# Attention with routed experts on one core: the packed chunks' splits on ScalarE and VectorE, and the value products put off by one unit

## The chip, the cores and the metric

The kernel runs on one core of a Trainium2 chip. The metric is device microseconds of one execution, the median of several runs; smaller is better. Beside the runs there is one profiled execution, whose trace gives every row shown below. Engines are TensorE (PE in the rows), VectorE (DVE), ScalarE (ACT), GpSimd (POOL) and SyncE (SP).

## What is computed

Attention over 4 batches, 8 heads, 576 positions of 64 numbers, mixed with a read of a memory matrix, and a mixture of experts over its 2304 output rows: 8 experts, of which each row takes two.

```python
scores = np.where(causal, -1e9, scale * q @ k.T);  a = softmax(scores);  local = a @ v
q_p = np.where(q > 0, q, np.exp(q) - 1.0) + 1.0
mem_out = (q_p @ M_prev) / ((q_p * z_prev).sum(-1) + 1e-06)
x = g * mem_out + (1 - g) * local                  # g = sigmoid(beta), rows of 512
logits = x @ w_gate + log1p(exp(x @ w_noise)) * noise
for each row: its two best experts e, softmax of the two logits as weights
out[row] += weight * (max(x[row] @ w1[e], 0) @ w2[e])
```

Products are made in pieces: a number is split into a rounded part ("hi") and what is left ("lo"), and hi·hi, lo·hi and hi·lo are added up.

## The kernel before

**Chunks and units.** The 576 positions of a batch are five chunks: i = 0 to 3 hold 128 rows of all 8 heads; i = 4 holds the last 64 rows and is *packed*: two heads share the 128 partitions. A chunk is worked off in units: two of four heads for i < 2, else four of two heads; 64 units in all. For a packed chunk the query parts are `q4h` and `q4l`; the key parts are the last 64 columns of `kT`, of which all the batch's later units read as well.

**One unit.** `score` multiplies queries and keys on TensorE (line 528, or 519 for a packed chunk), adds the mask, and takes the row maximum on VectorE (L538). `expo` takes the exponential on ScalarE (L559). `trans` turns the result `a` over on TensorE into a PSUM tile `tpa` (L577), up to four blocks to a tile, and ScalarE copies it to `aT` (L578). `av` multiplies `aT` with the values on TensorE (L599, `avT`, which uses half of the array's columns). After a chunk's last unit `out_copy` (L608, ScalarE) brings `avT` to `xo`, and `out_turn` turns it over (L635, `tpo`), scales it (L637) and adds the memory's part `xm` (L639) on VectorE.

**The loop over units.** Iteration u issues `expo(u+1)` and then mixes two lists. `ys` has the products and masks of `score(u+2)`, an `out_turn` that was put off, `av(u-1)` and perhaps an `out_copy`. `xs` has the preparation of later chunks, the routing of the finished ones and `trans(u)`. So each engine has one fixed order, on which it works in turn; an instruction that waits holds everything behind it on its engine.

**Preparation of a chunk.** `k_turn` and `q_turn` turn keys and queries over on TensorE (L409); ScalarE copies them to `kf` (L416) and `qf` (L441). For all but the first chunks GpSimd then makes the parts: the hi casts (L421 for `kT`, L452 for `qh` and `q4h`) and the lo subtractions (L422, L454). `mem` ends with the multiplication that gives `xm`, on GpSimd (L476).

**Routing.** When all of a batch's rows are known, `routing` finds each row's places in the experts' tables and puts ten indirect scatters of 16-byte rows on GpSimd's queue (L282, in a list `puts`). They are issued while the next batch is worked on, and on GpSimd's queue they stand directly ahead of the key parts of that batch's packed chunk. Batches 1, 2 and 3 have such scatters in front of their packed chunk; batch 0 has none.

**Experts.** From about 304 us on the experts' products (L906, L919) run on TensorE.

Of the kernel before, what the change touches and what calls it, by code (L numbers as in the profile page):

```python
# [9 lines left out]
F32 = mybir.dt.float32  # L10
# [5 lines left out]
ALU = mybir.AluOpType  # L16
# [3 lines left out]
P = 128  # L20
# [26 lines left out]
def tile_attention_moe(ctx: ExitStack, tc: tile.TileContext, q, k, v, M_prev, z_prev, beta,  # L47
                       w_gate, w_noise, noise, w1, w2, out):
    nc = tc.nc
# [269 lines left out]
    def attention():  # L319
        with ExitStack() as c2:  # L320
            ap_ = c2.enter_context(tc.tile_pool(name="ap", bufs=2))
# [70 lines left out]
            def prep(c):  # L392

                b, i = chunks[c]
                n = rows_of(i)
                d = CH.setdefault(c, {"b": b, "i": i, "n": n})
# [21 lines left out]

                def k_split():
                    hi, lo = keys()  # L420
                    (nc.gpsimd.tensor_copy if c > 1 else nc.scalar.copy)(hi, d["kf"])  # L421
                    nc.gpsimd.tensor_tensor(out=lo, in0=d["kf"], in1=hi.bitcast(F32), op=ALU.subtract)  # L422

                def turn_first(nm, g0):

# [21 lines left out]
                def q_split(part):  # L447
                    for j in ([0, 1] if i == 4 else [None]):
                        a = slice(0, P) if j is None else slice(j * 64, j * 64 + 64)
                        hi, lo = [d[nm][a, :, a] for nm in ("qh", "ql")]  # L450
                        if part == 0:
                            (nc.gpsimd.tensor_copy if c > 1 else nc.scalar.copy)(hi, d["qf"][a])  # L452
                        else:
                            nc.gpsimd.tensor_tensor(out=lo, in0=d["qf"][a], in1=hi.bitcast(F32), op=ALU.subtract)  # L454

                def q_min():
                    d["qpT"] = ap_.tile([P, 4, P], F32, tag="qpT", name="qpT", bufs=2)
# [2 lines left out]
                def mem(g0):  # L460
                    if g0 == 0:
                        d["xm"] = ap_.tile([P, H, D], F32, tag="xm", name="xm", bufs=4)
                    tp = ps_tp.tile([P, 512], F32, tag="tp", name="tpm")
                    v_ = tp[0:n, 0:4 * 65].rearrange("p (h e) -> p h e", e=65)
                    for g in range(2):
                        nc.tensor.matmul(tp[0:n, g * 130:(g + 1) * 130], d["qpT"][:, g0 + g, 0:n],
                                         mz[:, b, g0 + g].rearrange("p a e -> p (a e)"), start=True, stop=True)
                    m_ = ap_.tile([P, 4 * 65], F32, tag="mm", name="mm", bufs=3)
                    nc.scalar.copy(m_[0:n], tp[0:n, 0:4 * 65])
                    v_ = m_[0:n].rearrange("p (h e) -> p h e", e=65)  # L470
                    r = ap_.tile([P, 4, 1], F32, tag="mr", name="mr", bufs=4)
                    hs = slice(2 * g0, 2 * g0 + 4)
                    nc.vector.scalar_tensor_tensor(out=r[0:n], in0=v_[:, :, 64:65], scalar=1e-6, in1=ig[0:n, hs].unsqueeze(2),
                                                   op0=ALU.add, op1=ALU.mult)
                    nc.vector.reciprocal(r[0:n], r[0:n])
                    nc.gpsimd.tensor_tensor(out=d["xm"][0:n, hs, :], in0=v_[:, :, 0:64],  # L476
                                            in1=r[0:n].to_broadcast([n, 4, 64]), op=ALU.mult)

                mm = [lambda: mem(0), lambda: mem(2)]
# [11 lines left out]
            units = [(c, hs) for c in range(len(chunks)) for hs in units_of(chunks[c][1])]  # L491
# [72 lines left out]
            def trans(u):  # L564
                c, hs = units[u]
                i = CH[c]["i"]
                st = U[u]
                a = st["a"]
                aT = ap_.tile([P, 8, P], F32, tag="aT", name="aT", bufs=3)
                st["aT"] = aT  # L570
                nblk = len(hs) * (i + 1) if i < 4 else 5

                def bank(g):
                    w = min(4, nblk - g)
                    tp = ps_tp.tile([P, 512], F32, tag="tp", name="tpa")
                    for x_ in range(w):
                        nc.tensor.transpose(tp[:, x_ * P:(x_ + 1) * P], a[:, (g + x_) * P:(g + x_ + 1) * P], ident)  # L577
                    nc.scalar.copy(aT[:, g:g + w, :].rearrange("p b t -> p (b t)"), tp[:, 0:w * P])  # L578

                return [lambda g=g: bank(g) for g in range(0, nblk, 4)]  # L580

            def av(u):

                c, hs = units[u]
                d = CH[c]
                i, n = d["i"], d["n"]
                aT = U[u]["aT"]
                c0 = c - i

                def pairs():  # L590
                    if hs[0] == 0:
                        d["av"] = ps_av.tile([P, 512], F32, tag="avT", name="avT", bufs=1)
                    o_ = d["av"].rearrange("p (g t) -> p g t", g=4)
                    for h0 in sorted(h for h in hs if h % 2 == 0):
                        for j in range(i + 1):
                            for k_ in range(2):
                                x_ = hs.index(h0 + k_)
                                r_ = aT[:, j, x_ * 64:(x_ + 1) * 64] if i == 4 else aT[:, x_ * (i + 1) + j, :]
                                nc.tensor.matmul(o_[k_ * 64:(k_ + 1) * 64, h0 // 2, 0:n], CH[c0 + j]["v"][:, h0 + k_, :], r_,  # L599
                                                 start=(j == 0), stop=(j == i))  # L600
                return [pairs]
# [57 lines left out]
            NU = len(units)  # L659
# [63 lines left out]
                if c == 3:  # L723
                    late_consts()

            late = deque()
            for u in range(NU + 1):
                if u + 1 < NU:
                    expo(u + 1)
                ys = score(u + 2) if u + 2 < NU else []  # L730
                if u >= 1:
                    if late:
                        ys.append(late.popleft())
                    ys += av(u - 1)
                    cl = units[u - 1][0]
                    if u == NU or units[u][0] != cl:
                        ys.append(lambda cl=cl: out_copy(cl))
                        late.append(lambda cl=cl: out_turn(cl))
                xs = []
                if u < NU:  # L740
                    c, hs = units[u]
                    if u == first[c]:
                        on_chunk(c)
                    if chunks[c] == (B - 1, 4) and u == first[c]:
                        for f in range(2):
                            W0.append(load_w(None, 0, f, None, None, [
                                ap_.tile([P, H, D], F32, tag=nm + "n", name="w0" + nm, bufs=4) for nm in "kq"]))
                    if chunks[c] == (B - 1, 4) and u == first[c] + 1:
                        W0[:] = [split_w(ep, W0[0], "a", 1), split_w(ep, W0[1], "b", 1)]
                    if chunks[c][1] == 4 and (u + 1 == NU or units[u + 1][0] != c):  # L750
                        xs.append(lambda c=c: sums(c))
                    la = 4 if u < 3 else 7
                    nxt = units[u + la][0] if u + la < NU else -1
                    while any(f[0] <= nxt for f in fills):
                        xs.append(fills.popleft()[1])
                    while ev and ev[0][0] < TU[u + 1]:
                        xs.append(ev.popleft()[2])
                    for _ in range(1 if c < len(chunks) - 1 else 2):
                        if xq:
                            xs.append(xq.popleft())  # L760
                    if len(xq) > 2:
                        xs.append(xq.popleft())
                    if puts:
                        xs.append(lambda: puts and puts.popleft()())
                    xs += trans(u)
                    if puts:
                        xs.append(lambda: puts and puts.popleft()())
                nx, ny = len(xs), len(ys)
                done = 0
                for y, f in enumerate(ys):  # L770
                    f()
                    if small:
                        small.popleft()()
                    while done * ny < (y + 1) * nx:
                        xs[done]()
                        done += 1
                        if small:
                            small.popleft()()
                for f in xs[done:]:
                    f()  # L780
            d = CH[len(chunks) - 1]
            while late or xq:
                (late or xq).popleft()()
            return (list(small)
                    + xt_logits(d["b"], d["i"], d["x"].rearrange("p h d -> p (h d)")) + routing(B - 1, 3, 5))

# [408 lines left out]
```

## Time and profile before

| | |
|---|---|
| median of 3 runs | 773.23 us (770.99 to 773.27) |
| the profiled execution, its own time | 774.38 us |
| its span in the trace | 772.7 us |
| mean granted TensorE clock | 0.962 |
| busy in the span | PE 715.3 us (93%), DVE 418.0, ACT 371.3, POOL 366.2 |

The trace's span leaves out 1.7 us of the profiled execution's own time. That time is 1.15 us above the median. A granted clock of 1.00 is the higher of TensorE's two levels (2.4 GHz), 0.50 the lower (1.2 GHz); a value between them is a mean over a stretch.

### The profile page before, as it was taken

How to read it: one execution, taken by the hardware profiler on the slowest of the kernel's cores; microseconds unless marked ns; L12 is line 12 of the kernel's file. 1: busy time of each engine (PE TensorE's matmuls, PEld its weight loads, DVE VectorE, ACT ScalarE, POOL GpSimd, SP SyncE). 2: the span in 40 equal slices, each digit the busy share in tenths (PEclk: the TensorE clock that was granted, in tenths of full speed). 3: DMA queues.
4: the chain of work that ended last, by engine and by line, in shares of the span. 5: the costliest groups of instructions: out<-in, count | busy, mean ns of one | idle time of the engine just before them, and what ended most of it. 6: DMA issues, size and time to landing. Idle time of an engine off the chain costs nothing. (4 is left out here: it accounts for less than half of the span.)

```text
span 772.7 us, 14495 instructions
## 1 busy us (share of the span) xinstructions
PE 715.3 (93%) x5166; PEld 612.0 (79%) x5166; DVE 418.0 (54%) x1053; ACT 371.3 (48%) x951; POOL 366.2 (47%) x400
## 2 busy tenths in 40 slices
PE   6999996999699968878999999999999999999993
PEld 4678774877587757767888888988889988889882
DVE  3557583669377736826446454454554555455212
ACT  5588874787478744215415335234244244253210
POOL 6334527543664451555353572662752753724502
PEclk8799997999899989998999999999999999999998
DMA  9664421251120014659557465584683693864301
GB/s 166 89 131 98 106 73 37 63 103 55 36 78 21 16 57 130 152 93 241 164 118 178 144 165 147 174 176 122 184 207 99 191 228 115 208 142 151 93 0 61
DMA packets 165919, 92.95 MB, mean 120 GB/s; under 512 B 110564, under 2 KB 145380, under 8 KB 165840
## 3 DMA queue, kind: packets, MB, share of 16 engines
q1 hardware_dynamic: 155760, 72.97, 39.0%
q0 software_dynamic: 10080, 18.98, 9.8%
q8 instruction: 43, 0.70, 0.4%
q14 instruction: 36, 0.29, 0.1%
HBM read 69.68 MB, written 22.54 MB: 119 GB/s over the span
## 5 line engine op out<-in xcount | busy, mean ns | idle before, releaser
L868 POOL TENSOR_TENSOR w1lm<-w1sm,w1hm 128x512 fp32r<-128x512 f32 x63 | 82.3, 1308 | 134.0 <-DVE w1hm L867 72.7
L919 PE MATMUL y<-w2hm,hTh 128*128 128x512 f32 (+1 forms) x310 | 122.9, 397 | 0.0
L919 PE MATMUL y<-w2hm,hTl 128*128 128x512 f32 (+1 forms) x310 | 122.6, 396 | 0.0
L919 PE MATMUL y<-w2lm,hTh 128*128 128x512 f32 (+1 forms) x310 | 122.1, 394 | 0.0
L909 ACT ACTIVATE hTh<-ha 128x304 fp32r<-128x304 f32 (+2 forms) x64 | 27.2, 425 | 161.0 <-PE ha L906 138.9
L538 DVE TENSOR_REDUCE nb<-sc 128x1 f32<-128x384 f32 (+4 forms) x128 | 69.0, 554 | 55.1 <-PE sc L519 23.3
L869 ACT CAST w2hm<-w2sm 128x512 fp32r<-128x512 f32 x65 | 40.1, 619 | 100.1 <-PE y L919 100.1
L559 ACT ACTIVATE a<-sc,nb 128x128 f32<-128x128 f32 (+4 forms) x160 | 82.5, 530 | 1.2 <-DVE a L554 0.6
L870 DVE TENSOR_TENSOR w2lm<-w2sm,w2hm 128x512 fp32r<-128x512 f32 x65 | 48.5, 746 | 54.0 <-ACT w2hm L869 53.9
L578 ACT COPY aT<-tpa 128x512 f32<-128x512 f32 x120 | 60.5, 518 | 33.8 <-PE tpa L577 25.2
L867 DVE CAST w1hm<-w1sm 128x512 fp32r<-128x512 f32 x65 | 30.0, 462 | 79.1 <-PE hb L906 46.8
L906 PE MATMUL hb<-xTh,w1hm 128*128 128x304 f32 (+1 forms) x236 | 71.9, 305 | 0.0
L906 PE MATMUL ha<-xTl,w1hm 128*128 128x304 f32 (+1 forms) x236 | 71.9, 305 | 0.0
L906 PE MATMUL ha<-xTh,w1hm 128*128 128x304 f32 (+1 forms) x236 | 71.7, 304 | 0.0
L906 PE MATMUL ha<-xTh,w1lm 128*128 128x304 f32 (+1 forms) x236 | 71.3, 302 | 0.0
L906 PE MATMUL hb<-xTl,w1hm 128*128 128x304 f32 (+1 forms) x236 | 71.2, 302 | 0.0
L906 PE MATMUL hb<-xTh,w1lm 128*128 128x304 f32 (+1 forms) x236 | 71.0, 301 | 0.0
L919 PEld LDWEIGHTS y<-w2hm,hTl 128*128 128x128 f32 (+1 forms) x310 | 56.9, 184 | 15.6 <-DVE hTl L910 0.2
L577 PE MATMUL tpa<-identr,a 128*128 128x128 f32 x400 | 66.6, 287 | 1.5 <-ACT kf L416 0.8
L919 PEld LDWEIGHTS y<-w2lm,hTh 128*128 128x128 f32 (+1 forms) x310 | 57.1, 184 | 12.1
L919 PEld LDWEIGHTS y<-w2hm,hTh 128*128 128x128 f32 (+1 forms) x310 | 57.0, 184 | 11.3
L599 PE MATMUL avT<-aT,vt 128*64 128x128 f32 (+1 forms) x960 | 62.8, 268 | 0.4 <-ACT aT L578 0.4
(250 smaller groups left out, 1638.8 us busy)
## 6 DMA issues: line engine op xcount, KB each, us to landing
w1sm<-in_moe_w_dram SPq DMA_DIRECT2D x65, 256.0 KB
w2sm<-in_moe_w_dram SPq DMA_DIRECT2D x65, 256.0 KB
y_scratch<-o SPq DMA_DIRECT2D x21, 256.0 KB
vt<-in_v_dram SPq DMA_DIRECT2D x16, 256.0 KB
xall_scratch<-xr SPq DMA_DIRECT2D x16, 256.0 KB
kn<-in_k_dram SPq DMA_DIRECT2D x15, 256.0 KB
qn<-in_q_dram SPq DMA_DIRECT2D x15, 256.0 KB
y_scratch<-o SPq DMA_DIRECT2D x14, 224.0 KB
```

The lines of the kernel that those rows point to most:

```text
L538: nc.vector.tensor_reduce(out=nb[:, t * nh:(t + 1) * nh], in_=cols[t] if nh == 2 else cols[t][:, 0, :], axis=AX.X, op=ALU.max, negate=True)
L559: nc.scalar.activation(a[:, o:o + w], s_, AF.Exp, bias=st["nb"][:, x_:x_ + 1], accum_out=d["den"][:, at:at + 1])
L577: nc.tensor.transpose(tp[:, x_ * P:(x_ + 1) * P], a[:, (g + x_) * P:(g + x_ + 1) * P], ident)
L578: nc.scalar.copy(aT[:, g:g + w, :].rearrange("p b t -> p (b t)"), tp[:, 0:w * P])
L599: nc.tensor.matmul(o_[k_ * 64:(k_ + 1) * 64, h0 // 2, 0:n], CH[c0 + j]["v"][:, h0 + k_, :], r_, start=(j == 0), stop=(j == i))
L867: nc.vector.tensor_copy(h1, a)
L868: R["w1l"] = lo.tensor_tensor(out=l1, in0=a, in1=h1.bitcast(F32), op=ALU.subtract)
L869: nc.scalar.copy(h2, b_)
L870: nc.vector.tensor_tensor(out=l2, in0=b_, in1=h2.bitcast(F32), op=ALU.subtract)
L906: nc.tensor.matmul(o, w_[:, c, :], xT[xi][:, c, c0_:c1_], start=(c == 0 and i_ == 0), stop=(c == 3 and i_ == 2))
L909: R["hh"] = nc.scalar.activation(hT[0][:, c0_:c1_], o, AF.Relu)
L919: nc.tensor.matmul(ys[t][0:b_ - a_], hT[hi][:, a_:b_], w_, start=(f == 0 and i_ == 0), stop=(f == FF // P - 1 and i_ == 2))
```

## The change

1. For the packed chunks alone (i = 4, one in each batch) the hi casts of `kT` and `q4h` are made by ScalarE, the lo subtractions of `kT` and `q4l` and the multiplication for `xm` by VectorE. That is three casts (one of `kT`, two of `q4h`), three subtractions and two multiplications for each of the four packed chunks. The other chunks keep theirs on GpSimd.
2. Iteration u issues `av(u-2)` in place of `av(u-1)`, directly ahead of the products of `score(u+2)`, as one step that nothing is mixed into. `out_turn` comes at the end of the iteration in which its chunk's last values are multiplied. The loop has one more iteration, and `aT` four buffers in place of three.

```diff
                 def k_split():
                     hi, lo = keys()
-                    (nc.gpsimd.tensor_copy if c > 1 else nc.scalar.copy)(hi, d["kf"])
-                    nc.gpsimd.tensor_tensor(out=lo, in0=d["kf"], in1=hi.bitcast(F32), op=ALU.subtract)
+                    (nc.gpsimd.tensor_copy if c > 1 and i < 4 else nc.scalar.copy)(hi, d["kf"])
+                    (nc.gpsimd if i < 4 else nc.vector).tensor_tensor(out=lo, in0=d["kf"], in1=hi.bitcast(F32), op=ALU.subtract)
...
                         if part == 0:
-                            (nc.gpsimd.tensor_copy if c > 1 else nc.scalar.copy)(hi, d["qf"][a])
+                            (nc.gpsimd.tensor_copy if c > 1 and i < 4 else nc.scalar.copy)(hi, d["qf"][a])
                         else:
-                            nc.gpsimd.tensor_tensor(out=lo, in0=d["qf"][a], in1=hi.bitcast(F32), op=ALU.subtract)
+                            (nc.gpsimd if i < 4 else nc.vector).tensor_tensor(out=lo, in0=d["qf"][a], in1=hi.bitcast(F32), op=ALU.subtract)
...
-                    nc.gpsimd.tensor_tensor(out=d["xm"][0:n, hs, :], in0=v_[:, :, 0:64],
+                    (nc.gpsimd if i < 4 else nc.vector).tensor_tensor(out=d["xm"][0:n, hs, :], in0=v_[:, :, 0:64],
...
-                aT = ap_.tile([P, 8, P], F32, tag="aT", name="aT", bufs=3)
+                aT = ap_.tile([P, 8, P], F32, tag="aT", name="aT", bufs=4)
...
-            for u in range(NU + 1):
+            for u in range(NU + 2):
                 if u + 1 < NU:
                     expo(u + 1)
-                ys = score(u + 2) if u + 2 < NU else []
-                if u >= 1:
-                    if late:
-                        ys.append(late.popleft())
-                    ys += av(u - 1)
-                    cl = units[u - 1][0]
-                    if u == NU or units[u][0] != cl:
+                ys, end = [], []
+                if u >= 2:
+                    ys += av(u - 2)
+                    cl = units[u - 2][0]
+                    if u > NU or units[u - 1][0] != cl:
                         ys.append(lambda cl=cl: out_copy(cl))
-                        late.append(lambda cl=cl: out_turn(cl))
+                        end.append(lambda cl=cl: out_turn(cl))
+                if u + 2 < NU:
+                    ys += score(u + 2)
+                n_ = next((k_ for k_, f in enumerate(ys) if f.__name__ == "products"), len(ys) - 1) + 1
+                ys = [lambda fs=ys[:n_]: [f() for f in fs]] + ys[n_:] + end
```

The order on GpSimd, before, from the packed chunk of batch 1 to the first parts of batch 2 (`six` and `rows` are the scatters' places and data):

```order
L452 CAST q4h<-qf 64x4x64 x2
L454 TENSOR_TENSOR q4l<-qf,q4h 64x4x64 x2
L476 TENSOR_TENSOR xm<-mm,mr 128x256
L282 DMA tab_scratch<-rows,six 19456x4 x10
L421 CAST kT<-kf 128x4x64
L422 TENSOR_TENSOR kT<-kf,kT 128x4x64
L452 CAST qh<-qf 128x512
```

The same place on GpSimd, of the changed kernel:

```order
L421 CAST kT<-kf 128x4x128
L422 TENSOR_TENSOR kT<-kf,kT 128x4x128
L476 TENSOR_TENSOR xm<-mm,mr 128x256 x2
L282 DMA tab_scratch<-rows,six 19456x4 x10
L452 CAST qh<-qf 128x512
L454 TENSOR_TENSOR ql<-qf,qh 128x512
L452 CAST qh<-qf 128x512
```

Around the scatters no part of the packed chunk is left: behind them stand the parts of the next batch's first chunks.

The order on ScalarE, before, ahead of the packed chunk of batch 1, in the last units of the chunk before it (i = 3):

```order
L578 COPY aT<-tpa 128x512
L608 COPY xo<-avT 128x512
L578 COPY aT<-tpa 128x512
L559 ACTIVATE a,den<-sc,nb 128x512 x2
L416 ACTIVATE kf<-tpk 128x4x64
L578 COPY aT<-tpa 128x512 x2
L559 ACTIVATE a,den<-sc,nb 128x512 x2
```

The same place on ScalarE, of the changed kernel:

```order
L578 COPY aT<-tpa 128x512 x2
L559 ACTIVATE a,den<-sc,nb 128x512 x2
L608 COPY xo<-avT 128x512
L416 ACTIVATE kf<-tpk 128x4x64
L421 CAST kT<-kf 128x4x64
L578 COPY aT<-tpa 128x512 x2
L559 ACTIVATE a,den<-sc,nb 128x512 x2
```

The cast to `kT` stands behind the copies of `xo` and `kf` and ahead of the next two copies of `aT`; the subtraction stands on VectorE ahead of L637.

The order on TensorE, before, between the first and the second unit of batch 1's packed chunk:

```order
L577 MATMUL tpa<-identr,a 128x128 x4
L599 MATMUL avT<-aT,vt_128 64x128 x2
L599 MATMUL avT<-aT,vt_129 64x128 x2
L599 MATMUL avT<-aT,vt_130 64x128 x2
L599 MATMUL avT<-aT,vt_131 64x128 x2
L577 MATMUL tpa<-identr,a 128x128 x4
L519 MATMUL sc<-kT,q4h 128x288 x2
L519 MATMUL sc<-kT,q4l 128x288 x2
L519 MATMUL sc<-kT,q4h 128x288 x2
```

The same place on TensorE, of the changed kernel:

```order
L577 MATMUL tpa<-identr,a 128x128 x8
L599 MATMUL avT<-aT,vt_128 64x128 x2
L599 MATMUL avT<-aT,vt_129 64x128 x2
L599 MATMUL avT<-aT,vt_130 64x128 x2
L599 MATMUL avT<-aT,vt_131 64x128 x2
L519 MATMUL sc<-kT,q4h 128x288 x2
L519 MATMUL sc<-kT,q4l 128x288 x2
L519 MATMUL sc<-kT,q4h 128x288 x2
```

The second four turns stood between the values and the scores, and now stand with the first four; the values (of a unit earlier than before) lead straight into the scores.

## Rows read from the trace of the kernel before

**Rows 1.** The profile's first part: busy time, share of the span and number of instructions of each engine.

```profile
PE 715.3 (93%) x5166; PEld 612.0 (79%) x5166; DVE 418.0 (54%) x1053; ACT 371.3 (48%) x951; POOL 366.2 (47%) x400
```

**Rows 2.** The view of the waits, TensorE alone: what it waited for, us in total, times, the longest in us.

```profile
PE sc L519 <- POOL kT L421: 13.6, 2, 6.9
PE sc L519 <- issue: 7.3, 1, 7.3
...
PE avT L599 <- ACT aT L578: 0.4, 1, 0.4
```

**Rows 3.** The timeline of TensorE at the packed chunks of batches 1, 2 and 3 (three rows each): start, us, engine, line, operation, result and operands, tile, elements, count, and in brackets the idle time before it and who ended it. The first two rows of each are the first unit's first products, the third those of the second unit.

```profile
124.22 0.40 PE L519 MATMUL sc<-kT,q4h 128*128 128x288 f32 x1
131.87 0.61 PE L519 MATMUL sc<-kT,q4h 128*128 128x288 f32 x1 [7.26 <-issue]
138.13 0.51 PE L519 MATMUL sc<-kT,q4h 128*128 128x288 f32 x2
197.61 0.40 PE L519 MATMUL sc<-kT,q4h 128*128 128x288 f32 x1
204.78 0.61 PE L519 MATMUL sc<-kT,q4h 128*128 128x288 f32 x1 [6.77 <-POOL kT L421]
210.43 0.51 PE L519 MATMUL sc<-kT,q4h 128*128 128x288 f32 x2
269.63 0.40 PE L519 MATMUL sc<-kT,q4h 128*128 128x288 f32 x1
276.88 0.61 PE L519 MATMUL sc<-kT,q4h 128*128 128x288 f32 x1 [6.85 <-POOL kT L421]
282.81 0.51 PE L519 MATMUL sc<-kT,q4h 128*128 128x288 f32 x2
```

**Rows 4.** The timeline of GpSimd in the same three stretches: the first scatter of each, two later ones of batch 2, and the casts that follow the last.

```profile
118.97 1.19 POOL L282 DMA_INDIRECT tab_scratch<-rows,six  x1 [0.37 <-DVE nb L538]
131.41 0.41 POOL L421 CAST kT<-kf 128x256 fp32r<-128x256 f32 x1
191.65 1.03 POOL L282 DMA_INDIRECT tab_scratch<-rows,six  x1 [0.16 <-issue]
199.30 0.96 POOL L282 DMA_INDIRECT tab_scratch<-rows,six  x1 [0.30 <-issue]
200.56 1.35 POOL L282 DMA_INDIRECT tab_scratch<-rows,six  x1 [0.30 <-issue]
204.31 0.41 POOL L421 CAST kT<-kf 128x256 fp32r<-128x256 f32 x1
263.96 1.03 POOL L282 DMA_INDIRECT tab_scratch<-rows,six  x1 [0.16 <-issue]
276.42 0.41 POOL L421 CAST kT<-kf 128x256 fp32r<-128x256 f32 x1
```

**Rows 5.** The timeline of TensorE at the packed chunk of batch 0, which has no scatters in front of it: from the turns before its first scores to the second unit's.

```profile
59.17 0.61 PE L577 MATMUL tpa<-identr,a 128*128 128x128 f32 x4
59.61 0.60 PE L635 MATMUL tpo<-identr,xo 128*128 128x128 f32 x4
...
61.89 0.53 PE L519 MATMUL sc<-kT,q4h 128*128 128x288 f32 x2
...
63.72 0.60 PE L577 MATMUL tpa<-identr,a 128*128 128x128 f32 x4
64.25 1.09 PE L599 MATMUL avT<-aT,vt 128*64 128x128 f32 x16
...
65.69 0.52 PE L519 MATMUL sc<-kT,q4h 128*128 128x288 f32 x2
```

**Rows 6.** The timeline of ScalarE in the three stretches: the copy of the keys in batch 1, and of each batch the last copy of `aT` before the stall and the end of the exponentials that follow it.

```profile
122.16 0.39 ACT L416 ACTIVATE kf<-tpk 128x256 f32<-128x256 f32 x1
...
124.82 0.59 ACT L578 COPY aT<-tpa 128x512 f32<-128x512 f32 x1 [0.91 <-remote]
...
126.54 0.21 ACT L559 ACTIVATION_READ_ACCUMULATOR a<-sc,nb 128x1 f32 x1
201.02 0.59 ACT L578 COPY aT<-tpa 128x512 f32<-128x512 f32 x1 [2.96 <-remote]
...
202.75 0.21 ACT L559 ACTIVATION_READ_ACCUMULATOR a<-sc,nb 128x1 f32 x1
272.57 0.59 ACT L578 COPY aT<-tpa 128x512 f32<-128x512 f32 x1 [3.67 <-remote]
...
274.30 0.21 ACT L559 ACTIVATION_READ_ACCUMULATOR a<-sc,nb 128x1 f32 x1
```

**Rows 7.** The timeline of VectorE in batch 2's stretch: one of its additions, which reads two operands from SBUF.

```profile
200.38 0.69 DVE L639 TENSOR_TENSOR xr<-xr,xm 128x512 f32<-128x512 f32 x1
```

**Rows 8.** The view of stretches: length, busy us (and count) of PE, PEld, DVE, ACT and POOL, then the mean granted clock, the DMA share and GB/s. The first is the stretch that leads up to batch 0's packed chunk, the second to fourth go from the end of each stall to the second unit's scores, and the last from there in batch 3 to the experts.

```profile
46.72:61.89 15.17, 15.11 (x149) 11.37 (x147) 9.11 (x22) 12.19 (x35) 4.80 (x8) 1.00 0.57 113
...
131.87:138.13 6.26, 6.26 (x39) 5.68 (x39) 3.36 (x8) 2.29 (x4) 2.82 (x3) 0.56 0.11 24
...
204.78:210.43 5.65, 5.65 (x38) 5.07 (x39) 2.92 (x8) 2.29 (x4) 2.83 (x3) 0.62 0.12 26
...
276.88:282.81 5.93, 5.93 (x42) 5.04 (x43) 1.95 (x6) 1.32 (x3) 2.81 (x3) 0.67 0.25 72
282.81:304.32 21.51, 17.83 (x215) 14.80 (x214) 13.88 (x66) 13.19 (x41) 2.71 (x4) 1.00 0.29 93
```

More of the change, by code (lines that the diff above doesn't have):

```diff
@@ L724, in on_chunk @@
                     late_consts()
-            late = deque()
-            for u in range(NU + 1):
+            for u in range(NU + 2):
                 if u + 1 < NU:
                     expo(u + 1)
-                ys = score(u + 2) if u + 2 < NU else []
-                if u >= 1:
-                    if late:
-                        ys.append(late.popleft())
-                    ys += av(u - 1)
-                    cl = units[u - 1][0]
-                    if u == NU or units[u][0] != cl:
-                        ys.append(lambda cl=cl: out_copy(cl))
-                        late.append(lambda cl=cl: out_turn(cl))
+                ys, end = [], []
[3 more added lines that the diff above has]
+                    if u > NU or units[u - 1][0] != cl:
+                        ys.append(lambda cl=cl: out_copy(cl))
+                        end.append(lambda cl=cl: out_turn(cl))
[3 more added lines that the diff above has]
+                ys = [lambda fs=ys[:n_]: [f() for f in fs]] + ys[n_:] + end
                 xs = []
@@ L781, in attention @@
             d = CH[len(chunks) - 1]
-            while late or xq:
-                (late or xq).popleft()()
+            while xq:
+                xq.popleft()()
             return (list(small)
```

## The prediction

> **What bounds the kernel now.** I read the busy shares first: TensorE works 93% of the span, so time is gained where it stands still, or where its work becomes shorter; the others, at 47 to 54%, matter where TensorE waits for them [rows 1]. Next the waits of TensorE: one cause stands far above the rest, the scores of line 519 waiting for the cast to `kT` on GpSimd (13.6 us in two waits), and a third wait at the same line of 7.3 us put down to "issue" [rows 2]. The timeline shows what they are: once each in batches 1, 2 and 3, the first product of the packed chunk's first unit goes through and the second stands 7.26, 6.77 and 6.85 us, together 20.88 [rows 3]. GpSimd's timeline tells why. The cast starts at 131.41, 204.31 and 276.42, and TensorE goes on 0.46 or 0.47 us later each time; from 118.97, 191.65 and 263.96 until then GpSimd issues the previous batch's ten scatters, one every 1.26 us or so [rows 3, 4]. The keys were ready long before: `kf` of batch 1 was copied from 122.16 to 122.55, while the cast waited nine more microseconds in GpSimd's queue [rows 4, 6]. The "issue" of batch 1 is the same wait.
>
> The stall costs more than its idle time. In batch 0, without scatters, the packed chunk's second unit comes 65.69 - 61.89 = 3.80 us after the first [rows 5]. In batches 1 to 3 the distances are 13.91, 12.82 and 13.18 [rows 3], which is 10.11 + 9.02 + 9.38 = **28.5 us** too much. 20.9 of it is idle; the other 7.6 is the work behind the stall, done at a mean granted clock of 0.56 to 0.67, after 1.00 in an undisturbed stretch [rows 8]: TensorE had stood still, and the lower level held for part of these stretches.
>
> The second thing to see is that GpSimd's queue is not all that is late there. ScalarE's last copies of `aT` before the stall stood idle 0.91, 2.96 and 3.67 us for a releaser that the view calls remote, though TensorE had finished its turns and gone on [rows 6]. So while the scatters are issued, TensorE's finished work reaches the other engines late. Behind the stall this costs nothing today.
>
> **The change, part by part.** *Parts moved off GpSimd.* The first packed scores then need no instruction that stands behind the scatters: the order shows the cast on ScalarE right behind the copy of `kf`. In batch 1 it would end about 122.55 + 0.4 = 122.95, the subtraction on VectorE at most 0.7 later (the price of an addition twice its size, [rows 7]), so before 124.22. The stall goes: **-28.5**. Added are 12 casts of at most 0.39 (a copy of that size, [rows 6]), 4.7 us of ScalarE in all, and 12 subtractions and 8 multiplications of under 0.69 on VectorE. What hides them: before batch 0's packed chunk ScalarE is busy 12.19 of 15.17 us and VectorE 9.11, TensorE 15.11 [rows 8]; some 1.2 us more for ScalarE per chunk fit into its free 3. Cost 0; without that cover it would be up to 4.7.
>
> *What is late next.* Turns of the first packed unit's exponentials. In batch 0 they start 63.72 - 61.89 = 1.83 us after the first scores [rows 5]. The exponentials follow the late copies on ScalarE and end at 126.75, 202.96 and 274.51 [rows 6], that is 2.53, 5.35 and 4.88 us after the first scores [rows 3]. With the stall gone TensorE would wait 0.70 + 3.52 + 3.05 = 7.3 us for them. The scatters run on behind that point. The delays by then were 0.91 us, 5.85 after the first scatter; 2.96, 9.37 after; 3.67, 8.61 after. Grown in proportion to the scatters' end (12.44, 12.66 and 12.46 after their start, [rows 4]) they would be 1.9 + 4.0 + 5.3 = 11.2 us. I take **+9**, between the two; bounds are 0 (the second part of the change gives copies a unit more time, and a delay need not hold TensorE) and 18.5 (both sums, when the late exponentials and later copies each hold it).
>
> *Clock after these waits.* 20.9 us of idling gave 7.6 of slow work; in proportion 9 give 3.3. Against it: behind batch 3's stall TensorE is idle 21.51 - 17.83 = 3.7 us in all and its mean clock is still 1.00 [rows 8]. I take **+1.5**, between 0 and 3.3.
>
> *Value products put off.* They remove no wait: in the whole trace TensorE waits 0.4 us for `aT` ahead of them [rows 2]. The order is smoother: four turns step four times from row to row in 0.44 us when turns follow (59.17 to 59.61), but in 0.53 when value products follow, which use half the columns (63.72 to 64.25) [rows 5]: 0.09 for a change of shape. Counted over both orders, the attention stage has 275 such changes before and 264 after; 11 x 0.09 = **-1.0**, between 0 and twice that. The page "TensorEngine Tiling (Array Packing)" of the Trainium skill, section Tiling Modes, has it that a change of mode drains the engine; the trace's 0.09 us is what that could be here, and no larger price would follow from the page. The extra iteration issues nothing that was not issued before; the fourth `aT` only frees a wait. Nothing else is moved past SP's queue: the tables' load still follows the scatters, and behind them GpSimd's next parts are needed only a chunk later.
>
> *A rule against it.* The scatter at 200.56 took 1.35 us, its neighbour 0.96, and an addition with two SBUF operands ran on VectorE at 200.38 [rows 4, 7]. So of the two-operand steps that move to VectorE each may lengthen a scatter by 0.4 us; the kernel adds at most five for a chunk, 2 us of GpSimd's time, on which no scores wait any more. I count 0; if TensorE were held until the scatters' end, it would be up to 3 x 2 = 6, which lies within the 18.5. The Trainium skill's "GPSIMD Engine Reference", section Specifications, says that the SBUF interfaces are shared, with contention when a VectorE instruction has two SBUF inputs. The row agrees in this one case.
>
> **Sum.** On the profiled execution: 774.4 - 28.5 + 9 + 1.5 - 1.0 = 755.4; it lies 1.15 above the median of the runs, so **754** for the median.
>
> **Rivals.** *A, full gain.* Late signals do not hold TensorE, since it has other units' work: 774.4 - 28.5 - 1.0 - 1.15 = 744. For it: TensorE was busy 15.11 of 15.17 us ahead of batch 0's chunk [rows 8], with nothing to wait for. Against it: the exponentials' ends are read off, not guessed [rows 6].
>
> *C, the scatters keep holding.* Waits of 18.5 and slow work in proportion (18.5/20.9 x 7.6 = 6.7, halved for the row that speaks against it to 3.4): 774.4 - 28.5 + 18.5 + 3.4 - 1.0 - 1.15 = 766. For it: the delays grow while scatters are issued [rows 6], and every score, copy and turn of the packed units passes between engines. Against it: batch 1's is small, 0.91.
>
> *D, slower.* The cast now stands on ScalarE behind the copy of `xo`, which needs TensorE's signal. If that signal comes late by as much as the stall was long, the scores still wait for `kT`, and the 12 casts' 4.7 us lie on the path: 774.4 + 4.7 - 1.15 = 778. It decides from a delay of about 7 us; seen are 0.91 to 3.67 [rows 6], so this is unlikely.
>
> *E, no change.* Something else, such as the table load's or the experts' start, ends at a fixed time and gives the gain back: within 2.3 us of 773. Against it: behind the attention stage TensorE has its own work and no wait near that size [rows 2].
>
> **How the numbers follow.** The forecast, with its band of 748 to 760, gets 0.50; A 0.22; C 0.15; D 0.07; E 0.06. Below 742 lies a part of A (0.07), above 767 lie D, E and some of C (0.15): the range is 742 to 767. A difference of 0.3% (2.3 us) is about what a measurement of this kernel can tell from none. Faster by more: the forecast, A and C, 0.87; within it 0.06; slower 0.07.
>
> **What would show it.** The wait of line 519 for `kT` on GpSimd should be gone, and the packed chunks' second unit follow the first after 4 to 9 us in batches 1 to 3 and 3.8 in batch 0. New should be waits of the turns (L577) for ScalarE, near 1, 4 and 4 us, with remote releasers on ScalarE and VectorE while scatters run, and a granted clock of 0.8 or more behind them. If line 519 waits as long for L421 on ScalarE, D holds; if no wait stands in these stretches, A; if TensorE resumes only as the last scatter ends, C. I am wrong in the second part if chunks i = 0 to 3, away from scatters, grow longer or much shorter: they should change by 0.1 us each.

## The result and the profile after

The changed kernel takes 750.63 us, median of 3 runs (749.55 to 751.19), where the kernel before took 773.23: a ratio of 0.9715, with a 95% interval of 0.9683 to 0.9746. In a later session it was measured again at 748.74 (ratio 0.9686, 0.9648 to 0.9724). Its profiled execution has a span of 749.5 us, 23.2 less than before. The forecast was 754.

The first part of the profile after, answering to [rows 1]:

```profile
PE 708.7 (95%) x5166; PEld 605.5 (81%) x5166; DVE 423.2 (56%) x1073; ACT 375.7 (50%) x963; POOL 346.6 (46%) x368
```

GpSimd has 19.6 us less to do, ScalarE 4.4 and VectorE 5.2 more. The timeline of TensorE after, at the first and the second unit of the packed chunks of batches 1, 2 and 3, and at the first product of the experts (L907 here, L906 before), answering to [rows 3]:

```profile
128.24 0.54 PE L519 MATMUL sc<-kT,q4h 128*128 128x288 f32 x2
...
132.07 0.40 PE L519 MATMUL sc<-kT,q4h 128*128 128x288 f32 x1
...
191.69 0.53 PE L519 MATMUL sc<-kT,q4h 128*128 128x288 f32 x2
...
195.51 0.53 PE L519 MATMUL sc<-kT,q4h 128*128 128x288 f32 x2
...
257.23 0.53 PE L519 MATMUL sc<-kT,q4h 128*128 128x288 f32 x2
...
261.79 0.40 PE L519 MATMUL sc<-kT,q4h 128*128 128x288 f32 x1
...
282.84 0.66 PE L907 MATMUL ha<-xw,w1ha 128*128 128x384 f32 x2
```

The second unit follows after 3.83, 3.82 and 4.56 us, where it took 13.91, 12.82 and 13.18. All three stalls are gone, with the slow work behind them: 10.08 + 9.00 + 8.62 = **27.7 us**. The view of stretches shows TensorE busy throughout and the clock at 1.00 (it was 0.56, 0.62 and 0.67 behind the stalls, [rows 8]):

```profile
128.24:132.07 3.83, 3.83 (x41) 3.48 (x39) 2.75 (x9) 3.31 (x9) 2.92 (x4) 1.00 0.25 76
191.69:195.51 3.82, 3.82 (x41) 3.47 (x39) 2.74 (x9) 3.30 (x9) 2.90 (x4) 1.00 0.34 98
257.23:261.79 4.56, 4.56 (x46) 3.63 (x44) 2.69 (x8) 2.87 (x8) 3.34 (x5) 1.00 0.05 3
```

But the experts begin at 282.84 and not 27.7 us earlier than 304.32: the attention stage is 21.5 us shorter. The waits of TensorE after, answering to [rows 2], show what came in:

```profile
PE tpo L635 <- ACT xo L608: 2.5, 4, 0.8
PE tpl L161 <- DVE xTll L153: 2.4, 2, 1.9
PE tpa L577 <- ACT ll L170: 2.3, 2, 1.4
```

The same three in the view of the kernel before:

```profile
PE tpl L161 <- DVE xTll L153: 0.5, 1, 0.5
PE tpo L635 <- ACT xo L608: 0.5, 1, 0.5
...
PE tpa L577 <- ACT ll L170: 0.2, 1, 0.2
```

7.2 us against 1.2, so 6.0 more on these three rows. Other rows fell: L149 waits 1.1 us for `xr` in place of 2.4. The whole is in the view of stretches (columns as in [rows 8]), from 12 us to the experts, before and after:

```profile
12.00:304.32 292.32, 260.99 (x2600) 209.47 (x2600) 185.26 (x573) 206.94 (x624) 134.37 (x158) 0.94 0.33 73
12.00:282.84 270.84, 255.98 (x2605) 205.43 (x2605) 189.61 (x588) 212.28 (x637) 114.09 (x126) 0.98 0.36 80
```

TensorE is idle 31.3 us before, of which 20.9 are the three stalls, and 14.9 after. So outside the stalls it idles 4.4 us more. That leaves 1.8 of the 6.2 us by which the stage gained less than 27.7; they are longer work, whose cause was not followed. The places of the new waits, in the timelines of TensorE and VectorE after:

```profile
75.03 0.33 PE L577 MATMUL tpa<-identr,a 128*128 128x128 f32 x1 [0.95 <-ACT ll L170]
...
85.35 0.16 DVE L631 SCALAR_TENSOR_TENSOR ar<-dB,ib 64x4 f32<-64x4 f32 x1 [3.75 <-DMA dB<-d]
...
86.94 0.23 PE L161 MATMUL tpl<-xTll,wgs 128*16 128x128 f32 x1 [1.93 <-DVE xTll L153]
...
126.20 0.66 PE L635 MATMUL tpo<-identr,xo 128*128 128x128 f32 x4 [0.76 <-ACT xo L608]
```

The second part of the change makes them: with the first part alone (below) the three rows are 0.5, 0.5 and 0.7 us, with the second part alone 2.7, 1.0 and 3.2. `out_turn` now stands close behind its inputs: TensorE's turn waits for the copy `xo`, which stands on ScalarE behind a unit's exponentials; and after the packed chunk VectorE waits 3.75 us for the load of `dB` (the packed chunk's sums, which go through a DMA), with the routing's subtraction (L153) queued behind it, for which TensorE waits 1.93.

The last 1.7 us of the span's 23.2 came out of the experts' stage; they were not followed further.

### The profile page after: what moved, and what is told of

It reads as the page before. It is cut to its first block, busy times and chain, and to the rows that moved or that the text cites. A ratio compares the mean times of both kernels' runs of the same rounds, so it can differ in the third digit from the quotient of the medians.

```text
span 749.5 us, 14447 instructions
## 1 busy us (share of the span) xinstructions
PE 708.7 (95%) x5166; PEld 605.5 (81%) x5166; DVE 423.2 (56%) x1073; ACT 375.7 (50%) x963; POOL 346.6 (46%) x368
## 5 line engine op out<-in xcount | busy, mean ns | idle before, releaser
L907 PE MATMUL hb<-xTh,w1hm 128*128 128x304 f32 (+1 forms) x236 | 71.9, 305 | 0.0
L907 PE MATMUL ha<-xTh,w1hm 128*128 128x304 f32 (+1 forms) x236 | 71.2, 302 | 0.5 <-DVE hTl L911 0.5
L907 PE MATMUL ha<-xTl,w1hm 128*128 128x304 f32 (+1 forms) x236 | 71.3, 302 | 0.0
L907 PE MATMUL hb<-xTl,w1hm 128*128 128x304 f32 (+1 forms) x236 | 71.1, 301 | 0.0
L907 PE MATMUL hb<-xTh,w1lm 128*128 128x304 f32 (+1 forms) x236 | 70.8, 300 | 0.0
L907 PE MATMUL ha<-xTh,w1lm 128*128 128x304 f32 (+1 forms) x236 | 70.8, 300 | 0.0
L577 PE MATMUL tpa<-identr,a 128*128 128x128 f32 x400 | 61.2, 280 | 3.6 <-ACT ll L170 2.3
L599 PE MATMUL avT<-aT,vt 128*64 128x128 f32 (+1 forms) x960 | 64.6, 264 | 0.0
L578 ACT COPY aT<-tpa 128x512 f32<-128x512 f32 x120 | 58.5, 518 | 9.4 <-PE tpa L577 7.5
```

What stands on the lines that cost most here:

```text
L907: nc.tensor.matmul(o, w_[:, c, :], xT[xi][:, c, c0_:c1_], start=(c == 0 and i_ == 0), stop=(c == 3 and i_ == 2))
```

## Experiments

All have the kernel before measured beside them in the same session; its medians were 773.75, 773.65, 772.32 and 772.79.

### The two parts apart

The first part alone (all its edits, of which the diff shows the first), without anything of the loop over units:

```diff
-                    (nc.gpsimd.tensor_copy if c > 1 else nc.scalar.copy)(hi, d["kf"])
+                    (nc.gpsimd.tensor_copy if c > 1 and i < 4 else nc.scalar.copy)(hi, d["kf"])
...
             for u in range(NU + 1):
```

> The first part of the change alone: the packed chunks' parts on ScalarE and VectorE, the loop over units as before. Theory Q (all of the gain is that the cast to kT no longer stands behind the scatters; late signals belong to the stall and go with it): the three stalls go, 28 us, and the waits that the changed kernel has ahead of the packed chunks for xo and in the routing's small steps do not appear: 743 to 748 us, no remote releasers on ScalarE while scatters run. Rival S (scatters make TensorE's signals late whatever else runs, and putting the value products off is what hides it): TensorE waits for exponentials 0.7 to 5 us in each of the three packed chunks, 752 to 757 us.

Measured: 742.89 us, ratio 0.9616 (0.9588 to 0.9644), so 7.7 us less than the changed kernel. Its packed chunks' second units, in the timeline of TensorE:

```profile
122.47 0.53 PE L519 MATMUL sc<-kT,q4h 128*128 128x288 f32 x2
...
126.27 0.52 PE L519 MATMUL sc<-kT,q4h 128*128 128x288 f32 x2
```

3.80 us, the distance of batch 0, and 3.81 and 4.41 in the other two: 27.9 us less than before. Theory Q holds. The median gained 30.9 us, more than the stalls. In this trace the attention stage is 28.0 us shorter and the experts' stage 5.2, at a mean clock of 0.99 in place of 0.98; why it is shorter there was not followed.

The second part alone (the changed kernel with all edits of the first part taken back, of which the diff, against the changed kernel, shows the first):

```diff
-                    (nc.gpsimd.tensor_copy if c > 1 and i < 4 else nc.scalar.copy)(hi, d["kf"])
+                    (nc.gpsimd.tensor_copy if c > 1 else nc.scalar.copy)(hi, d["kf"])
...
             for u in range(NU + 2):
```

> The second part alone: value products put off by a unit and directly ahead of the scores, the parts on GpSimd as before. Theory Q: the three stalls of 7 us at line 519 stay, the waits for xo (some 2.5 us in all) and in the routing's steps (some 5) come on top, fewer changes of the array's shape take 1 to 4 off: 770 to 778 us. Rival V (the order of the value products carries a good part of the gain): 763 us or less, with the stalls shorter.

Measured: 779.04 us, ratio 1.0065 (1.0036 to 1.0094): a loss of about 5 us, just over Q's range; V is out. Its waits:

```profile
PE sc L519 <- POOL kT L421: 24.4, 3, 8.5
```

The three stalls are 2.8 us longer in all than the 21.6 us of the kernel before in its second profile (below). So the parts' costs are -31 and +5 apart, and the second adds 7 to 8 when the first is there.

### Is it the engine or the place in the queue?

Only the time at which a packed chunk's keys are prepared is moved; all parts stay on GpSimd:

```diff
-                for l, tb, te in ((qs, 17, 12), (ks_, 13, 8), (ps, 9, 1)):
+                for l, tb, te in ((qs, 17, 12), (ks_, *((22, 17) if chunks[c][1] == 4 else (13, 8))), (ps, 9, 1)):
```

> The kernel before with one number pair changed: the packed chunk's keys are turned and split some nine time units earlier, so that the cast to kT stands on GpSimd ahead of the ten scatters; all parts stay on GpSimd, the value products where they were. Theory Q (only the place in the queue counts, not the engine): the stalls go as with the first part alone, 743 to 749 us. Rival (GpSimd's load, or its work beside the scatters, is the cause, and the place in its queue only part): TensorE still waits there for other parts of GpSimd, 755 to 765 us.

Measured: 744.85 us, ratio 0.9626 (0.9596 to 0.9656), the median of 6 executions, of which one took 1703.39 us and the others 741.75 to 746.51. The timelines of GpSimd (the packed chunk's cast and the first of the ten scatters) and TensorE (first and second unit) in batch 1:

```profile
105.69 0.40 POOL L421 CAST kT<-kf 128x256 fp32r<-128x256 f32 x1 [1.57 <-ACT kf L416]
...
117.98 1.19 POOL L282 DMA_INDIRECT tab_scratch<-rows,six  x1 [0.37 <-DVE nb L538]
...
122.72 0.53 PE L519 MATMUL sc<-kT,q4h 128*128 128x288 f32 x2
...
126.52 0.38 PE L519 MATMUL sc<-kT,q4h 128*128 128x288 f32 x1
```

The cast now ends 11.9 us ahead of the scatters, and no stall is left: the second units come 3.80, 3.80 and 4.41 us after the first. And of the first part the keys' two steps alone, with the query parts and `xm` left on GpSimd:

```diff
-                    (nc.gpsimd.tensor_copy if c > 1 else nc.scalar.copy)(hi, d["kf"])
-                    nc.gpsimd.tensor_tensor(out=lo, in0=d["kf"], in1=hi.bitcast(F32), op=ALU.subtract)
+                    (nc.gpsimd.tensor_copy if c > 1 and i < 4 else nc.scalar.copy)(hi, d["kf"])
+                    (nc.gpsimd if i < 4 else nc.vector).tensor_tensor(out=lo, in0=d["kf"], in1=hi.bitcast(F32), op=ALU.subtract)
```

> Of the first part only the keys' two steps (cast and subtraction to kT); the query parts and the multiplications for xm stay on GpSimd, the loop as before. Theory Q (only what stands behind the scatters counts): the same time as the first part alone, 741 to 746 us. Rival (GpSimd's other parts of the packed chunk are late next): a wait of the scores for q4l or of VectorE for xm, 747 to 755 us.

Measured: 743.16 us, ratio 0.9597 (0.9567 to 0.9627). The three kernels are alike within their intervals. The gain is one cast that no longer stands behind ten scatters; on which engine it is made does not matter, and the other six moved steps of a packed chunk bring nothing that can be measured.

### Were the late signals real?

The prediction's +9 us stood on late releases ahead of the stalls [rows 6]. None is in the trace of the changed kernel, nor in those of the four kernels above. The kernel before was profiled once more:

> The kernel before, unchanged, profiled once more. If the late releases on ScalarE and VectorE ahead of the stalls (0.91, 2.96 and 3.67 us for a releaser called remote) belong to this kernel's order, they appear again with like sizes, as do the missing records; if they belong to that one execution, the rows stand without them, and the three stalls are longer by what ScalarE and TensorE then do earlier, 7 to 8.5 us each, at a like total near 773.

Measured: 774.09 us. The timelines of ScalarE and TensorE at batch 2, answering to the middle rows of [rows 6] and [rows 3]:

```profile
196.05 0.59 ACT L578 COPY aT<-tpa 128x512 f32<-128x512 f32 x1 [0.27 <-PE tpa L577]
...
197.78 0.21 ACT L559 ACTIVATION_READ_ACCUMULATOR a<-sc,nb 128x1 f32 x1
...
204.57 0.61 PE L519 MATMUL sc<-kT,q4h 128*128 128x288 f32 x1 [7.20 <-POOL kT L421]
```

The copy waits 0.27 us in place of 2.96, and the exponentials end 1.02 us after the first scores (196.97 in this trace) in place of 5.35. The stalls are 7.24, 7.20 and 7.20. So the late releases do not belong to this kernel's order of instructions alone: the same program ran with them and without.

### The second part's loss, and a session with late signals

Three kernels tried to say which half of the second part costs. The changed kernel with the turn put off by one iteration more:

```diff
-                        end.append(lambda cl=cl: out_turn(cl))
+                        late.append(lambda cl=cl: out_turn(cl))
```

> The changed kernel with out_turn at the end of the iteration after the one in which its chunk's last values are multiplied. If the waits of the turns for xo (0.76 us ahead of each of the three packed chunks' scores) and of VectorE for the load of the packed chunk's sums (1.9 us on TensorE near 85 us) come from the turn standing too close behind its inputs: 3 to 5 us off the changed kernel's 750.6, 746 to 748. Rival (the time is only moved, another of the routing's short chains is late next): 750 to 751.

Measured: 755.42 us, ratio 0.9775 (0.975 to 0.98), 5 us worse than the changed kernel. The waits for `xo` are down from 2.5 us to 0.5, but others took their place:

```profile
PE tpx L149 <- DVE xr L639: 5.8, 4, 2.4
```

It was 1.1 us in the changed kernel and 2.4 in the kernel before: the routing's first turn (L149) now waits for the later `out_turn`. The rival was right, and too mild. Putting the value products off without moving them in front of the scores (first part and four `aT` as in the change; the diff is against the first part alone):

```diff
-                if u >= 1:
+                if u >= 2:
                     if late:
                         ys.append(late.popleft())
-                    ys += av(u - 1)
-                    cl = units[u - 1][0]
+                    ys += av(u - 2)
+                    cl = units[u - 2][0]
```

> The first part of the change, and of the second only that the value products are put off by one unit (with the fourth aT); they stay in the place in the iteration where the kernel before has them, and so does out_turn. If the loss of the second part, 7 to 8 us against the first part alone (742.9), comes from putting off: 748 to 752 us. If it comes from the merged step in front of the scores and the turn at the iteration's end: 741 to 745 us.

Measured: 755.22 us, ratio 0.9754 (0.9725 to 0.9784): 12 us more than the first part alone, beyond either expectation. So putting off is what costs. That the changed kernel takes 5 us less is not shown to come from its place in front of the scores, since it also has the turn an iteration earlier. The kernel with the turn put off has the place in front and a late turn as here (at the end of the next iteration, here inside it), and takes as long (755.42). With a late turn, then, the place changes nothing that can be measured; with the place in front, the earlier turn gives 5 us back. A stretch without scatters agrees. From the scores of the second unit of chunk i = 0 of batch 2 to those of the last unit of chunk i = 3, the kernel with the turn put off takes 40.87 us and this one 40.63, where the changed kernel takes 38.13 (shown below):

```profile
144.40 0.33 PE L528 MATMUL sc<-kT,qh 64*128 64x128 f32 x2
...
185.27 0.50 PE L528 MATMUL sc<-kT,qh 64*128 64x512 f32 x2
```

```profile
149.50 0.33 PE L528 MATMUL sc<-kT,qh 64*128 64x128 f32 x2
...
190.13 0.50 PE L528 MATMUL sc<-kT,qh 64*128 64x512 f32 x2
```

The 12 us are not in waits. From 12 us to the experts, the first part alone and this kernel:

```profile
12.00:276.35 264.35, 251.92 (x2595) 201.79 (x2593) 191.67 (x592) 209.73 (x636) 115.46 (x126) 0.99 0.36 82
12.00:288.60 276.60, 264.66 (x2598) 207.42 (x2596) 186.79 (x593) 211.64 (x637) 119.17 (x126) 0.96 0.35 78
```

TensorE idles 12.4 us there and 11.9 here, and is busy 12.7 us longer. Two things are seen. The clock is lower: over the executions it is 0.979 to 0.986 with the first part alone (median 0.9815) and 0.971 to 0.978 here (median 0.974), by estimate 755 x 0.0075 = 5.7 us. And the array changes its shape more often: row by row of TensorE's timeline, 486 times up to the experts in place of 452 (441 in the changed kernel), by estimate, at the prediction's 0.09 us, 34 x 0.09 = 3 us. The rest is open. Two stretches (columns as in [rows 8]) show TensorE idle for 2.1 and 2.0 us and at a lower mean clock:

```profile
60.00:90.00 30.00, 27.92 (x294) 23.77 (x292) 19.06 (x53) 22.95 (x68) 11.83 (x12) 0.95 0.36 85
...
210.00:240.00 30.00, 28.00 (x301) 22.60 (x302) 22.08 (x53) 22.95 (x78) 16.81 (x19) 0.94 0.09 25
```

Then the copy to `xo` ahead of the exponentials, in the changed kernel:

```diff
-                if u + 1 < NU:
-                    expo(u + 1)
-                ys, end = [], []
                 if u >= 2:
-                    ys += av(u - 2)
+                    for f in av(u - 2):
+                        f()
...
-                        ys.append(lambda cl=cl: out_copy(cl))
+                        out_copy(cl)
                         end.append(lambda cl=cl: out_turn(cl))
+                if u + 1 < NU:
+                    expo(u + 1)
```

> The changed kernel, with the value products and the copy to xo issued ahead of the next unit's exponentials instead of behind them; the order on TensorE around the scores stays that of the changed kernel, on ScalarE the copy stands one or two exponentials earlier. If the changed kernel's loss against its first part alone (7 to 8 us) is in the turns' waits for xo, the waits shrink from 2.5 us to under 1 and the time falls to 747 to 749 us. If it lies mostly elsewhere (the routing's short chains, the start), 750 to 752 us.

Measured: 774.21 us over 12 runs (769.29 to 780.36), ratio 1.0022 (0.9992 to 1.0051); neither expectation. The timelines of POOL, TensorE, VectorE and ScalarE at batch 1's packed chunk:

```profile
122.04 1.19 POOL L282 DMA_INDIRECT tab_scratch<-rows,six  x1 [3.39 <-DVE rows L196]
...
126.88 0.43 PE L519 MATMUL sc<-kT,q4h 128*128 128x288 f32 x2
127.15 0.60 PE L409 MATMUL tpq<-identr,qn 128*128 128x128 f32 x4
...
134.25 1.11 PE L577 MATMUL tpa<-identr,a 128*128 128x128 f32 x4 [5.57 <-ACT qf L441]
...
130.75 0.46 DVE L538 TENSOR_REDUCE nb<-sc 128x1 f32<-128x288 f32 x1 [3.88 <-remote]
...
133.62 0.59 ACT L441 COPY qf<-tpq 128x512 f32<-128x512 f32 x1 [6.28 <-remote]
```

TensorE turned the queries until 127.75; ScalarE took note at 133.62. Scores that were done by 127.3 reached VectorE at 130.75. These are the late releases again, and here they hold TensorE: the second unit comes 10.97, 12.28 and 11.84 us after the first. In batch 2 the copy of the queries starts 7.2 us after their turns have ended. The other kernel of that session, with the value products in front of the scores but not put off, has late releases as well (the diff is against the changed kernel; `aT` has three buffers again):

```diff
-                    ys += av(u - 2)
-                    cl = units[u - 2][0]
+                    ys += av(u - 1)
+                    cl = units[u - 1][0]
```

> The first part of the change, and of the second only the place: the value products directly in front of the scores, but of the unit before (not put off), with three aT. If putting off is what the place needs, TensorE now waits for the copies of aT ahead of the value products, and the scores behind them are late too: 755 us or more, with waits for aT of over 10 us. If the place alone is good, 742 to 746 us.

Measured: 794.57 us, ratio 1.0296 (1.0259 to 1.0332). How much of it is the order and how much the late signals cannot be told apart in the total. But a stretch without scatters and late releases is longer too. From the second unit of chunk i = 0 of batch 2 to the second of chunk i = 3 it takes 33.88 us, against 31.68 in the kernel before and 31.64 with the first part alone:

```profile
162.35 0.33 PE L528 MATMUL sc<-kT,qh 64*128 64x128 f32 x2
...
196.23 0.49 PE L528 MATMUL sc<-kT,qh 64*128 64x512 f32 x2
```

TensorE waits 6.3 us for `aT` ahead of the value products in the whole trace, less than expected, where it waited 0.4. So in this stretch the place alone is a loss. The kernel with the copy to `xo` first was then run again, beside the changed kernel and the keys alone:

> The same kernel as the one with the copy to xo first, run again beside the changed kernel and the keys alone. Its waits of 7 to 8 us in the packed chunks of batches 1 to 3, behind signals of TensorE that reach ScalarE and VectorE 2 to 6 us late while scatters are issued, may belong to its order of instructions: then 774 us again, with late signals here and none in the two others. Or they belong to the state of the chip in that session, as the kernel before was profiled once with them and once without: then all three kernels have them, or none; without them 747 to 751 us here.

> The changed kernel, unchanged, in the same session. If late signals belong to an order of instructions: 750 to 752 us and none in its trace, whatever the kernel with the copy to xo first does. If they belong to the session and come again: 765 to 775 us, with waits of about 7 us in the first unit of the three packed chunks.

> The keys' two steps alone moved, the loop as before, in the same session. Without late signals 741 to 746 us as before. With them: if putting the value products off hides them, this kernel loses more than the changed one, 770 to 778 us; if it does not, both lose alike, 762 to 768 us here.

Measured in one session: 750.49 us (ratio 0.971, 0.9667 to 0.9753), 748.74 (0.9686, 0.9648 to 0.9724) and 741.50 (0.9616, 0.9581 to 0.965), without a late release in any of the three traces. The kernel with the copy to `xo` first, unchanged, has in place of the rows above:

```profile
127.71 0.59 ACT L441 COPY qf<-tpq 128x512 f32<-128x512 f32 x1 [0.44 <-PE tpq L409]
...
127.97 1.07 PE L577 MATMUL tpa<-identr,a 128*128 128x128 f32 x8
```

So late signals do not belong to an order of instructions alone, and where they came they cost this kernel 774.2 - 750.5 = 23.7 us. Nearly all of it lies in the packed chunks of batches 1 to 3: without late releases the second units come 3.82, 3.82 and 4.70 us after the first, 22.8 us less in all. What decides whether they come is not shown. The two sessions ran on different chips, on which the kernel before took 772.32 and 772.79; but the chip with the late signals gave seven traces without one in two earlier sessions, of other kernels. The kernel before shows no such cost: its two traced executions took 774.38 us with late releases and 774.09 without. A likely reason, not tested, is that its stall on GpSimd lasts until the last scatter anyway.

With the copy to `xo` first the waits for `xo` are 0.5 us in place of 2.5, and the time is that of the changed kernel within the intervals: these waits were not what the second part loses by.

Nothing here beats the first part, or the keys alone: 741 to 745 us in the four runs of the three kernels, against 749 to 751 for the changed kernel.

## Why the prediction was right, and where it was not

- **The stall** (-28.5): measured -27.7, and -27.9 with the first part alone. What removes it is the place in GpSimd's queue, as the prediction read it from [rows 3, 4]; the kernel with earlier keys shows that the change of engine is not needed.
- **The casts' cover** (0): right. ScalarE works 3.31 of 3.83 us in the packed unit after, TensorE all of them.
- **Late signals** (+9, bounds 0 to 18.5) and **clock behind them** (+1.5): 0 in both traces of the changed kernel. No wait stands in the packed units, which is the prediction's own sign for rival A. The step that failed is the one that took rows of a single execution for a property of the kernel: the mechanism was there when the rows were taken, but came up in only one of the later sessions. When it did, in a kernel that differs from the changed one in the order of a few steps, its price was 23.7 us with the clock, above the two upper bounds together (18.5 + 3.3).
- **Value products put off** (-1.0): wrong in sign; measured +7 to +8. "They remove no wait" was right; that they add none was not looked at. The turn, the sums' load and the routing's small steps lost their distance from what they wait for: 6.0 us on three rows, 4.4 more idling of TensorE in all. The rest is longer work, part of it at the lower clock. The smoother order exists: most of chunks 0 to 3 of batch 2, from the scores of one unit to those of another, took 38.91 us before, 38.87 with the first part alone and 38.13 after:

```profile
154.33 0.33 PE L528 MATMUL sc<-kT,qh 64*128 64x128 f32 x2
...
193.24 0.50 PE L528 MATMUL sc<-kT,qh 64*128 64x512 f32 x2
```

```profile
148.54 0.33 PE L528 MATMUL sc<-kT,qh 64*128 64x128 f32 x2
...
186.67 0.50 PE L528 MATMUL sc<-kT,qh 64*128 64x512 f32 x2
```

  That is 0.8 us for a batch's four chunks where no such wait stands, 0.2 for a chunk, where 0.1 was forecast; it is less than the waits take.
- **Two-operand steps lengthening scatters** (0, up to 0.4 us each): in the changed kernel 11 scatters ran beside one for 0.3 us or more; 9 took 0.90 to 0.96 us and 2 took 1.17 and 1.47. The row at 200.56 [rows 4] was no rule.

That the total came out right was luck: two errors stood against each other, 10.5 us of lateness that did not come, and 8 to 9 us between the -1.0 for the second part and what it cost. Rival A, at 744, describes the kernel that the first part alone makes.

What stays open: when late signals come; why putting the value products off lengthens TensorE's work, of which clock and shape changes explain a part; and why the experts' stage became shorter.

## What to carry to other kernels

A step of 0.4 us that the bound engine waits for must not stand behind ten DMA issues on an in-order queue; moving it ahead of them in time works as well as moving it to another engine. When a change joins two edits, measure each: here one gave all of the gain and the other took a quarter of it back. Before a term of a sum rests on waits with no visible cause, profile the same kernel a second time.

## What the runs showed of the hardware

While GpSimd issues indirect scatters, ScalarE and VectorE can take up finished work of TensorE up to about 7 us late, with a releaser that the view calls remote. This was so in some sessions and not in others: in the first profile of the kernel before and in both traces of one session, and in none of the eleven other traces, with the same scatters at the same pace (mostly 0.96 us each, 0.30 between). Two programs, the kernel before and the one with the copy to `xo` first, were traced both ways; the two sessions of the latter were on different chips.
